# Feed-forward square on VectorE, an order planned with traced durations, and filler matmuls ahead of the feed-forward

## The chip, the cores and the metric

The kernel runs on one core of a Trainium2 chip. The metric is the device time of one execution in microseconds (us). The core's engines are called by the profile's names: PE (TensorE's matmul) and PEld (its weight load), DVE (VectorE), ACT (ScalarE), POOL (GpSimd), SP (SyncE, which here issues the DMAs).

## The reference

Thresholded attention over 8 batches of 8 heads (576 positions, head dimension 64), whose output is the input of a gated feed-forward layer with token shift (model width 512, hidden width 1024). q, k and v are float32, the feed-forward's weights float64.

```python
def _attn_ref(q, k, v, tau):
    scale = 1.0 / np.sqrt(q.shape[-1])
    scores = scale * np.matmul(q, k.transpose(0, 1, 3, 2))
    thresh = np.max(scores, axis=-1, keepdims=True) - tau
    scores = np.where(scores >= thresh, scores, -1000000000.0)
    scores = scores - np.max(scores, axis=-1, keepdims=True)
    attn = np.exp(scores)
    attn = attn / (np.sum(attn, axis=-1, keepdims=True) + 1e-09)
    return np.matmul(attn, v).astype(np.float32)

def _moe_ref(x, mu_k, mu_r, w_k, w_v, w_r):
    B, S, D = x.shape
    x_prev = np.concatenate([np.zeros((B, 1, D), dtype=np.float32), x[:, :-1, :]], axis=1)
    xk = mu_k * x + (1.0 - mu_k) * x_prev
    xr = mu_r * x + (1.0 - mu_r) * x_prev
    k = np.maximum(xk @ w_k, 0.0)
    v = k * k @ w_v
    r = 1.0 / (1.0 + np.exp(-(xr @ w_r)))
    return (r * v).astype(np.float32)
```

## The kernel before

**The plan.** The kernel doesn't issue instructions in the order in which its Python loops meet them. Each piece of work is a step, given to `add` with its engine, its cost (`occ`, how long the engine is held; `lat`, how long until the result can be used, `occ + 0.1` if not given), what it reads and writes, a priority `key` and a name `kind`. `Plan.order` then lays all steps out in a simulated time: at each turn it takes, over all engines, the step that can start earliest, and among steps of one engine that could start together the one with the smallest key. `Plan.issue` emits the instructions in that order, so that each engine's queue is fixed by the plan, while semaphores guard the data. The plan's numbers set only the order, and no engine waits for a planned time.

The key of a step is shifted by `NUDGE[kind]`, and by `FIRST[kind]` too while the key is below `UNTIL` (60). `HOP` is the planned delay from one engine to another, `LATE` an extra delay for the score and attention matmuls after `FROM` (200 us planned), `AHEAD` how far their keys are put forward. `CHUNK` and `FETCH` model PE's instruction fetch: 3.55 us for each 256 instructions.

**Attention.** A job is one pair of heads of one batch, 32 in all. `operands` loads rq, rk and v (L455 on) and makes the split operands qa, qb and kc: each float32 value is kept as a rounded part and the remainder. A job has five units (four of 128 queries by two heads, and "T" for the 64 queries left over of both heads). For a unit, `scores` runs the score matmuls into a PSUM tile `s` (L562, L578; three such tiles), and `softmax` takes the negated row maximum on DVE (L624, L632), the threshold on ACT (L640, Prelu with a huge slope), the exponential and its sum on ACT (L648), the reciprocal on DVE (L656, L657) and the normalisation on POOL (L671). `turn` transposes on DVE (L688, L692), and `attend` multiplies with v on PE in three groups of 96 small matmuls (L717), again into `s` tiles, which ACT copies into xT and xE (L743, L750).

**Weights.** `weight` makes 20 pieces (8 of w_k, 4 of w_r, 8 of w_v) during the first jobs: a DMA of 512 KB of float64 words on SP, an ACT pass (L397), four DVE passes that pick the bits together (L405 `dve5`, L419 `dve6`, L426 `dve7`, L436 `dve8`), an ACT copy (L443) and a POOL subtraction for the remainder (L447). `W0 + W1 * j` is the earliest planned time of the DMA of piece j of the first eight, `W2` of all later ones.

**Feed-forward.** `ffn_chunk` works on 256 positions: 18 chunks, two per batch and two for the left-over positions of four batches each. A chunk makes xk and xr (POOL subtraction L816, DVE scaling L825, ACT copy L838, POOL remainder L846), multiplies xk with w_k in four groups of 24 matmuls (L868, into one of the two PSUM tiles `w`), takes Relu (L876, ACT), the square (L877, ACT), its rounded part (L881, ACT) and remainder (L891, POOL) into k2; it multiplies xr with w_r (L910), applies the sigmoid on ACT (L914, L918), multiplies k2 with w_v (L932), and multiplies both on DVE (L938) before the output DMA. Tiles `r` (two) hold the intermediate values, and `k2` and `sg` exist once.

The square and its neighbours on ACT:

```python
add("ACT", 0.49, lambda r=r, h=h: A.activation(r.get(), h.get().rearrange("p a b -> p (a b)"), AF.Relu), reads=[h], writes=[r], key=key - 20, kind="act11")
add("ACT", 0.53, lambda r=r: A.activation(r.get(), r.get(), AF.Square), writes=[r], key=key - 1, kind="act12")
```

Of the kernel before, what the change touches and what calls it, by code (L numbers as in the profile page):

```python
# [7 lines left out]
F32 = mybir.dt.float32  # L8
FR = mybir.dt.float32r
# [40 lines left out]
class Plan:  # L50
# [3 lines left out]
    HOP, LATE, FROM, AHEAD = 0.05, 0.05, 200.0, 65.0  # L54
    SOFT = {"DVE": 0, "ACT": 0}
    NUDGE = {
# [7 lines left out]
    }  # L64
    FIRST, UNTIL = {
# [8 lines left out]
    CHUNK, FETCH = 256, 3.55  # L74
# [62 lines left out]
    def order(self, loose=()):  # L137
# [24 lines left out]
        code, turned = 0, -100.0  # L162
        out = []
# [86 lines left out]
    def issue(self):  # L250
        for i in self.out:
            self.steps[i].fn()
# [3 lines left out]
def tile_threshold_attention_then_rwkv_ffn(  # L256
# [45 lines left out]
    W0, W1, W2, W3, AVK = 3.220, 2.801, 34.671, 0.000, 1.0  # L302
# [67 lines left out]

    pieces = {}

    def weight(j, name, w, c, f, key, wait):
# [8 lines left out]
        def t():  # L382
            return xT[1].get()[:, col, 1 : 1 + 512]
# [12 lines left out]
            0.56,  # L396
# [3 lines left out]
            key=key, kind="act1",  # L400
# [3 lines left out]
            0.4,  # L404
            lambda: V.tensor_scalar(t(), t(), W_MIN, W_MAX, op0=ALU.max, op1=ALU.min),  # L405
            writes=box,
            key=key, kind="dve5",
# [5 lines left out]
        def word(y):  # L413
# [4 lines left out]
            0.4,  # L418
            lambda: V.tensor_scalar(u(), u(), 0x07FFFFFF, 3, op0=ALU.bitwise_and, op1=ALU.logical_shift_left),  # L419
            writes=box,  # L420
            key=key, kind="dve6",
# [3 lines left out]
            0.65,  # L425
# [5 lines left out]
            key=key, kind="dve7",  # L431
# [3 lines left out]
            0.65,  # L435
# [5 lines left out]
            key=key, kind="dve8",  # L441
        )
        add("ACT", 0.53, lambda: A.activation(piece.get()[:, 0], t(), AF.Copy), reads=box, writes=[(piece, 0)], key=key, kind="act2")  # L443
        add(
            "POOL",
            1.27,
# [3 lines left out]
            key=key, kind="pool1",  # L450
# [4 lines left out]
    def operands(job, key):  # L455
        b, hp = job["b"], job["hp"]
        job["st"] = []
        for h in range(2):
# [20 lines left out]
                0.62,  # L479
# [3 lines left out]
                key=key - PREP, kind="act4",  # L483
# [9 lines left out]
                key=key - PREP, kind="pool2",  # L493
# [3 lines left out]
                0.7,  # L497
# [5 lines left out]
                key=key - PREP, kind="act3",  # L503
# [3 lines left out]
                0.8,  # L507
# [10 lines left out]
                key=key - PREP, kind="dve7b",  # L518
# [13 lines left out]
    def scores(unit, ss, key):  # L532
# [5 lines left out]
        if unit["kind"] == "T":  # L538

            for v_ in range(2):  # L540
                for h in range(2):

                    def tail(v_=v_, h=h):
# [6 lines left out]
                        0.26,  # L550
# [3 lines left out]
                        key=key - 3, kind="act5",  # L554
# [33 lines left out]
    def softmax(unit):  # L588
# [16 lines left out]
        for y in ys:  # L605
# [12 lines left out]
            def col(j, y=y):  # L618
# [4 lines left out]
                0.67,  # L623
# [3 lines left out]
                key=key - KMAX, kind="dve9",  # L627
# [3 lines left out]
                0.1,  # L631
# [3 lines left out]
                key=key - KMAX, kind="dve10",  # L635
# [3 lines left out]
                0.625,  # L639
# [3 lines left out]
                key=key - KEXP, kind="act6",  # L643
# [3 lines left out]
                0.70,  # L647
# [3 lines left out]
                key=key - KMASK, kind="act7",  # L651
# [3 lines left out]
        def invert():  # L655
# [5 lines left out]
            0.29,  # L661
# [3 lines left out]
            key=n + 0.5, kind="dve11",  # L665
        )
        for y in ys:
            add(
                "POOL",
                0.715,  # L670
                lambda y=y: G.tensor_scalar(  # L671
                    part(y), part(y), sm.get()[:, 3, y : y + 1], 0.0, op0=ALU.mult, op1=ALU.add
                ),
                reads=[(sm, (3, y))],
                writes=[p[y]],
                key=n - 1.0, kind="pool3",
            )
# [4 lines left out]
    def turn(unit):  # L682
# [11 lines left out]
        if unit["kind"] == "P":  # L694
            add("DVE", 1.27, main, writes=[(sq, (c, 0)), (sq, (c, 1))], key=n - 1.0, kind="dve12")
        else:
            add("DVE", 0.7, tail, writes=[(sq, (c, 1))], key=n - 1.0, kind="dve13")

    def attend(job, key):
# [39 lines left out]
        for a in range(2):  # L739
# [16 lines left out]
            add("ACT", 0.3, put, reads=[os[a]], writes=main, key=key - 5, kind="act8")  # L756
            add("ACT", 0.1, put_tail, reads=[os[a]], writes=tail, key=key - 5, kind="act9")
# [15 lines left out]
    def ffn_chunk(kind, b0, g, key):  # L773
# [35 lines left out]
        for hc in range(0, NCT, 2):  # L809
# [9 lines left out]
            for j in range(2):  # L819
                d = sbuf("r", [P, 2, CH], F32, 2)  # L820

                def scale(j=j, d=d, diff=diff, hc=hc):
# [18 lines left out]
                    key=key, kind="act10",  # L841
# [9 lines left out]
                    key=key, kind="pool6",  # L851
# [4 lines left out]
        for j in range(NFT // 2):  # L856
            h = psum("w", [P, 2, CH], NF)
            for f in range(2):
# [17 lines left out]
            add("ACT", 0.49, lambda r=r, h=h: A.activation(r.get(), h.get().rearrange("p a b -> p (a b)"), AF.Relu), reads=[h], writes=[r], key=key - 20, kind="act11")  # L876
            add("ACT", 0.53, lambda r=r: A.activation(r.get(), r.get(), AF.Square), writes=[r], key=key - 1, kind="act12")  # L877
            add(
                "ACT",
                0.53,  # L880
# [5 lines left out]
                key=key - 1, kind="act13",  # L886
# [9 lines left out]
                key=key - 1, kind="pool7",  # L896
# [3 lines left out]
        for j in range(CH // P):  # L900
# [13 lines left out]
            add("ACT", 0.49, lambda j=j, z=z: A.activation(sg.get()[:, j], z.get(), AF.Copy), reads=[z], writes=[(sg, j)], key=key - 20, kind="act14")  # L914
        add(
            "ACT",
            3.6,
            lambda: A.activation(sg.get(), sg.get(), AF.Sigmoid),  # L918
            writes=[(sg, 0), (sg, 1)],
            key=key - 1, kind="act15",  # L920
        )
        for j in range(CH // P):
            ts = slice(j * P, (j + 1) * P)
            vps = psum("w", [P, DM], NF)
            for ft in range(NFT):
# [15 lines left out]
                key=key - 20, kind="dve15",  # L941
# [100 lines left out]
```

## Time and profile before

| what | value |
|---|---|
| median of three runs | 1008.28 us (1006.56 to 1009.07) |
| profiled execution | 1007.83 us, span 1005.8 us |
| PE busy | 900.2 us (90%), 13520 matmuls |
| ACT busy | 794.9 us (79%) |
| DVE busy | 705.8 us (70%) |
| POOL busy | 588.6 us (59%) |
| mean granted PE clock | 0.948 |

A group's row names its line, engine, operation, output and input, and then gives the busy time, the mean of one in ns, the idle time of the engine just before these instructions, and what ended it. A row of waits gives the waiting engine and line, the releaser, us in total, times and the longest. A row of the timeline gives start, duration, engine, line, operation and how many were merged, with the idle time before it in brackets. An engine that isn't the bottleneck may be idle at no cost.

### The profile page before, as it was taken

The numbers are of one execution on the slowest core, as the hardware profiler recorded it, in microseconds if no ns is written. First come the engines' busy times: TensorE is split into PE (matmuls) and PEld (weight loads), VectorE is DVE, ScalarE is ACT, GpSimd is POOL, SyncE is SP. The second block draws the span as 40 slices with busy tenths as digits, with TensorE's granted clock in tenths as the row PEclk, the third lists the DMA queues.
The fourth block names the chain that finished last, engine by engine and source line by source line (L and its number), as shares of the span: only waits on it lengthen the run. The fifth ranks groups of instructions, "written<-read, shape, count | busy, mean of one in ns | idle before, by whom it ended". The sixth has DMA issues, their size and how long they took to land.

```text
span 1005.8 us, 32052 instructions
## 1 busy us (share of the span) xinstructions
PE 900.2 (90%) x13520; PEld 790.3 (79%) x13520; DVE 705.8 (70%) x1434; ACT 794.9 (79%) x1660; POOL 588.6 (59%) x576
## 2 busy tenths in 40 slices
PE   3355669899989999999999999999999999999988
PEld 3244558798878988898889798888888888889876
DVE  5979999677878686868686958686858677741130
ACT  5766878788889898989898798888898979854422
POOL 1756667665656665756565657565666657543431
PEclk9577778899999999999999999999999999999999
DMA  7562231233323232333222223332322222210001
GB/s 282 179 252 82 89 105 50 72 117 103 110 96 117 96 117 96 117 97 103 98 99 91 77 76 117 96 117 84 118 72 89 94 90 73 70 49 22 22 22 22
DMA packets 31599, 97.48 MB, mean 97 GB/s; under 512 B 3808, under 2 KB 3808, under 8 KB 27360
## 3 DMA queue, kind: packets, MB, share of 16 engines
q1 hardware_dynamic: 31456, 95.44, 28.1%
q8 instruction: 106, 1.74, 0.7%
q14 instruction: 37, 0.30, 0.1%
HBM read 85.99 MB, written 9.44 MB: 95 GB/s over the span
## 4 chain that ended last, share of the span: by engine, by line
PE 43%; DVE 9%; ACT 4%; POOL 3%; issue 2%; ACTq 0%; DVEq 0%; POOLq 0%
PE w L868 13%; PE s L717 8%; PE w L932 7%; PE w L910 7%; PE s L578 6%; DVE r L825 3%; DVE sm L624 2%; DVE sq L688 2%; PE s L562 2%; POOL sq L671 1%; POOL xk L846 1%; ACT sq L640 1%; ACT sq L648 1%; ACT L648 1%; DVE sm L656 1%
## 5 line engine op out<-in xcount | busy, mean ns | idle before, releaser
L671 POOL TENSOR_SCALAR sq<-sq,sm 128x576 f32<-128x576 f32 x288 | 239.4, 843 | 162.4 <-DVE sm L657 90.6
L624 DVE TENSOR_REDUCE sm<-s 128x1 f32<-128x576 f32 x288 | 211.9, 745 | 81.6 <-PE s L578 75.7
L640 ACT ACTIVATE sq<-s,sm 128x576 f32<-128x576 f32 x288 | 206.4, 737 | 59.2 <-DVE sm L632 55.5
L868 PE MATMUL w<-xk,wk 128*128 128x256 f32 x1728 | 228.8, 285 | 4.0 <-ACT xk L838 2.3
L868 PEld LDWEIGHTS w<-xk,wk 128*128 128x128 f32 x1728 | 217.7, 191 | 9.6 <-issue 4.2
L648 ACT ACTIVATE sq<-sq,small 128x576 f32<-128x576 f32 x288 | 222.9, 777 | 2.0
L932 PE MATMUL w<-wv,k 128*128 128x512 f32 x864 | 215.2, 394 | 0.0
L688 DVE STREAM_TRANSPOSE sq<-sq 128x1152 f32<-128x1152 f32 x128 | 175.5, 1371 | 54.8 <-POOL sq L671 54.5
L717 PE MATMUL s<-sq,v 32*64 32x144 f32 x9216 | 177.8, 292 | 19.2 <-issue 8.4
L717 PEld LDWEIGHTS s<-sq,v 32*64 32x64 f32 x9216 | 151.0, 133 | 44.2 <-issue 23.8
L932 PEld LDWEIGHTS w<-wv,k 128*128 128x128 f32 x864 | 157.8, 188 | 32.5 <-issue 3.6
L578 PE MATMUL s<-kc,qa 128*128 128x288 f32 x512 | 128.4, 334 | 50.3 <-ACT sq L640 37.6
L578 PEld LDWEIGHTS s<-kc,qa 128*128 128x128 f32 x512 | 88.7, 204 | 78.0 <-ACT sq L640 35.2
L488 POOL TENSOR_TENSOR kc<-rk,kc 64x576 fp32r<-64x576 f32 x64 | 96.8, 1517 | 82.0 <-issue 60.8
L846 POOL TENSOR_TENSOR xk<-r,xk 128x512 fp32r<-128x512 f32 x72 | 95.3, 1324 | 83.8 <-ACT xk L838 82.8
L578 PE MATMUL s<-kc,qb 128*128 128x288 f32 x512 | 117.7, 314 | 0.0
L891 POOL TENSOR_TENSOR k<-r,k 128x512 fp32r<-128x512 f32 x72 | 93.2, 1298 | 40.1 <-ACT k L881 38.1
L910 PE MATMUL w<-wr,xk 128*128 128x512 f32 x432 | 107.1, 393 | 0.0
L825 DVE SCALAR_TENSOR_TENSOR r<-r,mu_sb,xT 128x256 f32<-128x256 f32 x128 | 73.9, 618 | 37.9 <-POOL xk L846 22.3
L578 PEld LDWEIGHTS s<-kc,qb 128*128 128x128 f32 x512 | 89.5, 205 | 1.2 <-issue 1.2
L910 PEld LDWEIGHTS w<-wr,xk 128*128 128x128 f32 x432 | 78.9, 189 | 14.5 <-ACT r L876 0.3
L838 ACT ACTIVATE xk<-r 128x512 fp32r<-128x512 f32 x72 | 45.2, 628 | 54.6 <-DVE r L825 54.3
(53 smaller groups left out, 915.2 us busy)
## 6 DMA issues: line engine op xcount, KB each, us to landing
v<-in_v SPq DMA_DIRECT2D x32, 1152.0 KB, 5.1
rq<-in_qk SPq DMA_DIRECT2D x64, 288.0 KB, 2.9
rk<-in_qk SPq DMA_DIRECT2D x64, 288.0 KB, 2.9
out<-sg SPq DMA_DIRECT2D x32, 256.0 KB, 2.1
wk<-in_w_k SPq DMA_DIRECT2D x8, 512.0 KB, 7.9
wv<-in_w_v SPq DMA_DIRECT2D x8, 512.0 KB, 10.5
wr<-in_w_r SPq DMA_DIRECT2D x4, 512.0 KB, 6.5
out<-sg SPq DMA_DIRECT2D x8, 128.0 KB, 2.4
```

Of the source, the lines that this page charges most:

```text
L578: PE.matmul(ss[y].get()[:, z, 0:HS], l.get()[:, c * P : (c + 1) * P], r.get()[:, keys(z)], start=(j == 0), stop=(j == 1),)
L624: lambda sv=sv, col=col: V.tensor_reduce(col(0), sv(), axis=AX.XY, op=ALU.max, negate=True),
L640: lambda st=st, pv=pv, col=col: A.activation(pv(), st(), AF.Prelu, bias=col(1), alpha=STEEP),
L648: lambda y=y, col=col: A.activation(part(y), part(y), AF.Exp, bias=small.get()[:, 3:4], accum_out=col(2)),
L671: lambda y=y: G.tensor_scalar(part(y), part(y), sm.get()[:, 3, y : y + 1], 0.0, op0=ALU.mult, op1=ALU.add),
L688: V.transpose(t, t)
L717: PE.matmul(os[a // 2].get()[hs, a % 2, 0:NX], vt.get()[rows, j, hs], sq.get()[rows, j, h], start=(j == 0), stop=(j == NB - 1),)
L825: V.scalar_tensor_tensor(d.get()[:, y, o : o + n], diff.get()[:, y, o : o + n], mu_sb.get()[:, j, hc + y : hc + y + 1], prv[:, hc + y], op ...
L846: lambda j=j, d=d, cs=cs: G.tensor_tensor(mix[j].get()[:, 1, cs], d.get(), mix[j].get()[:, 0, cs].bitcast(F32), op=ALU.subtract),
L868: PE.matmul(h.get()[:, f], l, r, start=(ct == 0 and i == 0), stop=(ct == NCT - 1 and i == 2))
L910: PE.matmul(z.get(), l, r, start=(ct == 0 and i == 0), stop=(ct == NCT - 1 and i == 2))
L932: PE.matmul(vps.get(), l, r, start=(ft == 0 and i == 0), stop=(ft == NFT - 1 and i == 2))
```

## The change

1. The square of the hidden values is a DVE product `r * r` (kind `dve16`) in place of an ACT activation.
2. The planned costs of many steps, `NUDGE`, `FIRST`, `LATE`, `AHEAD` and the planned times of the weight DMAs are set anew, so the order on every engine differs. Each weight's ACT and DVE passes, for example, now have a `lat` of their own.
3. Wherever the plan leaves PE idle for more than 0.3 us and no `w` tile has been used yet, it counts how many matmuls of 0.12 us fit in the gap; `issue` emits as many filler matmuls (128x128 by 128x256, all ones) at that place in PE's queue. They write to a tile `waste`, which lies where the second `w` tile will be.

```diff
-    HOP, LATE, FROM, AHEAD = 0.05, 0.05, 200.0, 65.0
+    HOP, LATE, FROM, AHEAD = 0.05, 0.1, 200.0, 70.0
     NUDGE = {
-        "act1": -59.5, "act10": 67.0, "act11": -222.0, "act12": -115.0, "act13": 59.5, "act14": -52.5, "act15": 165.0,
...
+        "act1": -76.0, "act10": 42.5, "act11": -241.5, "act12": -115.0, "act13": 28.5, "act14": -15.5, "act15": 189.0,
...
-    CHUNK, FETCH = 256, 3.55
+    CHUNK, FETCH, FILL = 256, 3.55, 0.12
...
+        self.fill = {}
...
             s.start = t
+            if e == "PE" and not turn["w"] and t - free[e] > 0.3:
+                self.fill[len(out)] = int((t - free[e]) / self.FILL)
...
     def issue(self):
-        for i in self.out:
+        for k, i in enumerate(self.out):
+            for _ in range(self.fill.get(k, 0)):
+                self.filler()
             self.steps[i].fn()
...
-    W0, W1, W2, W3, AVK = 3.220, 2.801, 34.671, 0.000, 1.0
+    W0, W1, W2, W3, AVK = 4.655, 3.665, 50.033, 0.000, 1.0
...
+    one = const.tile([P, CH], FR, name="one")
+    V.memset(one.bitcast(F32), 1.0)
+    waste = ps.tile([P, 512], F32, tag="w_1", name="waste", bufs=1)
+    plan.filler = lambda: PE.matmul(waste[:, 0:CH], one[:, 0:P], one, start=True, stop=True)
...
-            0.4,
+            0.333,
...
-            key=key, kind="dve5",
+            key=key, lat=0.42, kind="dve5",
...
-            0.4,
+            0.333,
...
-            key=key, kind="dve6",
+            key=key, lat=0.43, kind="dve6",
...
-            0.65,
+            0.6,
...
-            key=key, kind="dve7",
+            key=key, lat=0.69, kind="dve7",
...
-            0.65,
+            0.6,
...
-            key=key, kind="dve8",
+            key=key, lat=0.68, kind="dve8",
...
-            add("ACT", 0.49, ... AF.Relu), ... kind="act11")
-            add("ACT", 0.53, lambda r=r: A.activation(r.get(), r.get(), AF.Square), writes=[r], key=key - 1, kind="act12")
+            add("ACT", 0.478, ... AF.Relu), ... lat=0.6, kind="act11")
+            add("DVE", 0.6, lambda r=r: V.tensor_tensor(r.get(), r.get(), r.get(), op=ALU.mult), writes=[r], key=key - 1, lat=0.69, kind="dve16")
...
```

More of the change, by code (lines that the diff above doesn't have):

```diff
@@ L395, in weight @@
             "ACT",
-            0.56,
+            0.558,
             lambda: A.activation(t(), words.get()[:, :, 1].bitcast(F32), AF.Abs),
@@ L399, in weight @@
             writes=box,
-            key=key, kind="act1",
+            key=key, lat=0.67, kind="act1",
         )
@@ L440, in weight @@
             writes=box,
-            key=key, kind="dve8",
+            key=key, lat=0.68, kind="dve8",
         )
-        add("ACT", 0.53, lambda: A.activation(piece.get()[:, 0], t(), AF.Copy), reads=box, writes=[(piece, 0)], key=key, kind="act2")
+        add("ACT", 0.52, lambda: A.activation(piece.get()[:, 0], t(), AF.Copy), reads=box, writes=[(piece, 0)], key=key, lat=0.63, kind="act2")
         add(
             "POOL",
-            1.27,
+            1.24,
             lambda: G.tensor_tensor(piece.get()[:, 1], t(), piece.get()[:, 0].bitcast(F32), op=ALU.subtract),
@@ L449, in weight @@
             writes=[(piece, 1)],
-            key=key, kind="pool1",
+            key=key, lat=1.28, kind="pool1",
         )
@@ L478, in operands @@
                 "ACT",
-                0.62,
+                0.575,
                 lambda rk=rk, both=both: A.activation(both.get(), rk.get(), AF.Copy),
@@ L482, in operands @@
                 writes=[both],
-                key=key - PREP, kind="act4",
+                key=key - PREP, lat=0.68, kind="act4",
             )
@@ L492, in operands @@
                 writes=[both],
-                key=key - PREP, kind="pool2",
+                key=key - PREP, lat=1.44, kind="pool2",
             )
@@ L496, in operands @@
                 "ACT",
-                0.7,
+                0.667,
                 lambda rq=rq, top=top: A.activation(
@@ L502, in operands @@
                 writes=[top],
-                key=key - PREP, kind="act3",
+                key=key - PREP, lat=0.78, kind="act3",
             )
@@ L506, in operands @@
                 "DVE",
-                0.8,
+                0.726,
                 lambda rq=rq, top=top, low=low: V.scalar_tensor_tensor(
@@ L517, in operands @@
                 writes=[low],
-                key=key - PREP, kind="dve7b",
+                key=key - PREP, lat=0.81, kind="dve7b",
             )
@@ L549, in scores @@
                         "ACT",
-                        0.26,
+                        0.147,
                         tail,
@@ L626, in softmax @@
                 writes=[(sm, (0, y))],
-                key=key - KMAX, kind="dve9",
+                key=key - KMAX, lat=0.75, kind="dve9",
             )
@@ L634, in softmax @@
                 writes=[(sm, (1, y))],
-                key=key - KMAX, kind="dve10",
+                key=key - KMAX, lat=0.2, kind="dve10",
             )
@@ L642, in softmax @@
                 writes=[p[y]],
-                key=key - KEXP, kind="act6",
+                key=key - KEXP, lat=0.74, kind="act6",
             )
@@ L660, in softmax @@
             "DVE",
-            0.29,
+            0.28,
             invert,
@@ L664, in softmax @@
             writes=[(sm, (3, y)) for y in ys],
-            key=n + 0.5, kind="dve11",
+            key=n + 0.5, lat=0.47, kind="dve11",
         )
@@ L669, in softmax @@
                 "POOL",
-                0.715,
+                0.72,
                 lambda y=y: G.tensor_scalar(
@@ L675, in softmax @@
                 writes=[p[y]],
-                key=n - 1.0, kind="pool3",
+                key=n - 1.0, lat=0.76, kind="pool3",
             )
@@ L694, in turn @@
         if unit["kind"] == "P":
-            add("DVE", 1.27, main, writes=[(sq, (c, 0)), (sq, (c, 1))], key=n - 1.0, kind="dve12")
+            add("DVE", 1.292, main, writes=[(sq, (c, 0)), (sq, (c, 1))], key=n - 1.0, lat=1.38, kind="dve12")
         else:
-            add("DVE", 0.7, tail, writes=[(sq, (c, 1))], key=n - 1.0, kind="dve13")
+            add("DVE", 0.69, tail, writes=[(sq, (c, 1))], key=n - 1.0, lat=0.77, kind="dve13")
     def attend(job, key):
@@ L754, in put_tail @@
                 )
-            add("ACT", 0.3, put, reads=[os[a]], writes=main, key=key - 5, kind="act8")
-            add("ACT", 0.1, put_tail, reads=[os[a]], writes=tail, key=key - 5, kind="act9")
+            add("ACT", 0.265, put, reads=[os[a]], writes=main, key=key - 5, lat=0.39, kind="act8")
+            add("ACT", 0.077, put_tail, reads=[os[a]], writes=tail, key=key - 5, lat=0.2, kind="act9")
     def edge(b, key):
@@ L875, in ffn_chunk @@
             r = sbuf("r", [P, 512], F32, 2)
-            add("ACT", 0.49, lambda r=r, h=h: A.activation(r.get(), h.get().rearrange("p a b -> p (a b)"), AF.Relu), reads=[h], writes=[r], key=key - 20, kind="act11")
-            add("ACT", 0.53, lambda r=r: A.activation(r.get(), r.get(), AF.Square), writes=[r], key=key - 1, kind="act12")
+            add("ACT", 0.478, lambda r=r, h=h: A.activation(r.get(), h.get().rearrange("p a b -> p (a b)"), AF.Relu), reads=[h], writes=[r], key=key - 20, lat=0.6, kind="act11")
+            add("DVE", 0.6, lambda r=r: V.tensor_tensor(r.get(), r.get(), r.get(), op=ALU.mult), writes=[r], key=key - 1, lat=0.69, kind="dve16")
             add(
                 "ACT",
-                0.53,
+                0.52,
                 lambda r=r, js=js: A.activation(
@@ L885, in ffn_chunk @@
                 writes=[(k2, (0, j))],
-                key=key - 1, kind="act13",
+                key=key - 1, lat=0.63, kind="act13",
             )
@@ L895, in ffn_chunk @@
                 writes=[(k2, (1, j))],
-                key=key - 1, kind="pool7",
+                key=key - 1, lat=1.3, kind="pool7",
             )
@@ L913, in ffn_chunk @@
                 add("PE", 0.69, mm, reads=[w, *([xr] if ct == 0 else [(xr, (0, c2)), (xr, (1, c2))])], writes=[z, *([(sg, j)] if ct == 0 else [])], key=key, lat=0.86, kind="pe7", ni=6)
-            add("ACT", 0.49, lambda j=j, z=z: A.activation(sg.get()[:, j], z.get(), AF.Copy), reads=[z], writes=[(sg, j)], key=key - 20, kind="act14")
+            add("ACT", 0.478, lambda j=j, z=z: A.activation(sg.get()[:, j], z.get(), AF.Copy), reads=[z], writes=[(sg, j)], key=key - 20, lat=0.6, kind="act14")
         add(
             "ACT",
-            3.6,
+            3.55,
             lambda: A.activation(sg.get(), sg.get(), AF.Sigmoid),
             writes=[(sg, 0), (sg, 1)],
-            key=key - 1, kind="act15",
+            key=key - 1, lat=3.65, kind="act15",
         )
@@ L940, in ffn_chunk @@
                 writes=[(sg, j)],
-                key=key - 20, kind="dve15",
+                key=key - 20, lat=0.68, kind="dve15",
             )
```

16 lines of the change are left out of this document (8 added, 8 removed), and 27 rows, old and new, of the table NUDGE.

## The prediction, made before the changed kernel ran

> **What bounds the kernel now.** I read the stages first: busy time of each engine by stretch. The cut at 153 us is where the first feed-forward matmul (L868) runs, and the cut at 900 where attention is nearly over. The columns are the stretch, its length, busy us of PE, PEld, DVE, ACT and POOL, the granted clock, the DMA share and GB/s.
>
> ```profile
> 0.00:153.00 153.00, 77.64 (x1366) 64.89 (x1367) 133.90 (x253) 110.76 (x236) 83.80 (x80) 0.73 0.46 163
> 153.00:200.00 47.00, 43.43 (x672) 38.27 (x671) 37.61 (x74) 38.88 (x82) 35.51 (x32) 0.89 0.18 62
> 200.00:900.00 700.00, 681.94 (x10757) 601.61 (x10755) 515.83 (x1056) 608.59 (x1284) 433.59 (x431) 1.00 0.29 96
> 900.00:1006.00 106.00, 97.24 (x731) 85.50 (x729) 18.42 (x54) 36.69 (x60) 35.70 (x35) 0.97 0.07 21
> ```
>
> There are two regimes. Up to 153 us DVE is busy 88% of the time and PE only 51%, at a granted clock of 0.73. From 200 us on PE is busy 97% at full clock, with 18.1 us idle in 700. So a gain has three places: an earlier start of the feed-forward, the 18.1 us, and PE's 8.8 us idle in the last stretch. Anything else falls on engines that wait for PE. The second view is who waits for whom, for PE up to 153 us (two lines), for DVE there (one), for PE from 200 to 900 us (six) and at the end (two).
>
> ```profile
> PE s L578 <- ACT sq L640: 32.5, 18, 9.3
> PE s L717 <- issue: 6.7, 4, 3.9
> ...
> DVE sm L624 <- PE s L578: 10.0, 5, 5.0
> ...
> PE s L578 <- ACT sq L640: 5.1, 9, 0.9
> PE s L717 <- ACT sq L640: 4.5, 4, 2.2
> PE s L578 <- ACT xT L743: 2.4, 5, 0.8
> PE s L717 <- ACT r L877: 2.2, 1, 2.2
> PE s L717 <- issue: 1.2, 2, 1.0
> PE s L717 <- ACT sq L648: 0.9, 1, 0.9
> ...
> PE w L868 <- ACT xk L838: 2.3, 1, 2.3
> PE w L868 <- POOL xk L846: 1.7, 2, 1.0
> ```
>
> Early on, PE's waits are for PSUM tiles that DVE and ACT free, so they are DVE's pace seen from PE. Only where DVE itself waits for PE (10.0 us of its 19.1 idle) does PE's speed count. The largest of these is in the timeline, with two bursts of the attention product for the clock:
>
> ```profile
> 47.90 3.13 PE L717 MATMUL s<-sq,v 32*64 32x144 f32 x96
> 429.25 1.78 PE L717 MATMUL s<-sq,v 32*64 32x144 f32 x96
> 59.98 0.46 PE L717 MATMUL s<-sq,v 32*64 32x144 f32 x4 [3.93 <-issue]
> 61.21 0.76 DVE L624 TENSOR_REDUCE sm<-s 128x1 f32<-128x576 f32 x1 [4.97 <-PE s L578]
> ```
>
> The same 96 matmuls take 3.13 us at the half clock that follows an idle stretch, and 1.78 us in the dense stage. DVE's hole of 4.97 us stands behind such a burst and behind 3.93 us of PE waiting for its own instructions.
>
> **The change part by part.** The sum is against the profiled execution: 1007.83 us, its span 1005.8 and 2.0 around it; the median of the runs, 1008.28, lies 0.45 above.
>
> *Fillers.* Their price is that of the feed-forward's equal shape, dense and full clock against cold:
>
> ```profile
> 911.52 11.58 PE L868 MATMUL w<-xk,wk 128*128 128x256 f32 x96
> 922.95 5.63 PE L910 MATMUL w<-wr,xk 128*128 128x512 f32 x24
> 152.60 1.48 PE L868 MATMUL w<-xk,wk 128*128 128x256 f32 x6
> 154.13 0.85 PE L578 MATMUL s<-kc,qa 128*128 128x288 f32 x2
> ```
>
> From start to the next start that is 11.43/96 = 0.119 us warm, which is the plan's 0.12, and 1.53/6 = 0.255 cold. PE's real work up to 153 us is about 77.64 x 0.73 = 57 us at full clock, so some 96 us of gaps hold about 800 fillers, 1600 instructions with their weight loads. As long as they end before the real step's operand is there they cost nothing; what covers them is DVE. Their gain lies in DVE's waits for PE. Bounds: 10.0 us gained if all of them go, and a loss that I price under the rivals. I take half, -5, because the largest wait is part clock (3.13 against 1.78) and part instruction fetch, which a full clock doesn't help. The clock also still stands at 0.73 when the feed-forward begins, and at 0.70 in a second cold stretch:
>
> ```profile
> 152.60:160.00 7.40, 7.35 (x45) 7.05 (x45) 6.71 (x18) 6.53 (x17) 5.83 (x6) 0.73 0.21 76
> 180.00:190.00 10.00, 7.06 (x28) 6.16 (x27) 6.00 (x14) 4.89 (x14) 6.16 (x6) 0.70 0.19 63
> ```
>
> Here PE is busy throughout, so the first gives 7.35 x 0.27 = 2.0 us; fillers end with the first feed-forward matmul, so the second (2.1 us) stays. -2. The plan counts its fetch chunks of 256 without the fillers, so the four fetch waits (6.7 us) fall elsewhere: between -6.7 and +6.7, taken as 0, since nothing in the rows favours either phase. The tile `waste` lies in a feed-forward PSUM slot, and whatever follows in it is PE's own, in order. The memset of `one` is half the size of this one, and DVE then waits for a transfer anyway:
>
> ```profile
> 0.97 0.48 DVE L363 MEMSET bd<- 128x512 f32 x1
> 3.31 0.15 DVE L331 TENSOR_SCALAR small<-small 128x1 f32<-128x1 f32 x1 [1.85 <-DMA small<-in_tau]
> ```
>
> It costs nothing; without that cover about 0.25 us.
>
> *Square from ACT to DVE.* The rows: the square on ACT, a DVE product with one operand in PSUM, and two DVE operations with two operands in SBUF (min/median/max in ns where three numbers stand).
>
> ```profile
> L877 ACT ACTIVATE r<-r 128x512 f32<-128x512 f32 x72 | 45.4, 630 | 0.6
> L938 DVE TENSOR_TENSOR sg<-w,sg x36: 643/678/693, 200.5 to 1001.2; 128x512 f32<-128x512 f32 x36
> L825 DVE SCALAR_TENSOR_TENSOR r<-r,mu_sb,xT x128: 443/479/1660, 94.6 to 941.4; 128x256 f32<-128x256 f32 x128
> L825 DVE SCALAR_TENSOR_TENSOR r<-r,mu_sb,xT 128x256 f32<-128x256 f32 x128 | 73.9, 618 | 37.9 <-POOL xk L846 22.3 <-POOL r L816 15.6
> L436 DVE SCALAR_TENSOR_TENSOR xT<-wk,xT x8: 669/682/1881, 25.5 to 84.2; 128x512 uint32<-128x512 uint32 x8
> L436 DVE SCALAR_TENSOR_TENSOR xT<-wk,xT 128x512 uint32<-128x512 uint32 x8 | 6.8, 846 | 0.0
> ```
>
> ACT loses 72 x 0.630 = 45.4 us. A DVE product of this size takes 0.678 us, and operations with both operands in SBUF are now and then stretched: L825 has a mean of 0.618 over a least of 0.443, 0.175 more or 1.4 times, L436 0.846 over 0.669. L938, with one operand in PSUM, never is. The square reads r twice from SBUF. Its price lies between 0.678 (no stretch) and 0.678 x 1.4 = 0.95; I take 0.678 + 0.175 = 0.85, since L436, the same width, shows that much added. 72 of them are 61 us, where the plan counts 0.6 each, 43. The feed-forward runs from 153 to 1006, so 700/853 of the 72, about 59, fall between 200 and 900 us. There ACT goes from 87% to (608.6 - 59 x 0.63)/700 = 82%, DVE from 74% to (515.8 + 59 x 0.85)/700 = 81%. Of PE's 18.1 us idle there 15.1 end with ACT. Bounds: all of them gained, or as much again added, because DVE's queue is in order and a square waiting for its Relu holds the reductions behind it, which hold ACT. I take -7 for about half of ACT's and +3 for DVE's: -4. The chain Relu, square, copy, low half gains one more change of engine; its cover is the gate's product (L910, 5.63 us a chunk) between the last L868 group and L932, while the chain without its last piece, Relu, square and copy, is about 0.63 + 0.85 + 0.63 = 2.1 us, taking ACT's two at L877's price; so 3 us are left for the low half on POOL.
>
> The Trainium skill, SBUF — State Buffer, section Who interferes with whom, says that a VectorE instruction with two SBUF inputs contends with a GpSimd instruction reading SBUF; the trace agrees (L436 up to 1881 ns, L938 never over 693). By the plan's 0.6 the DVE share would be 79%, by the stretched row 81%; either leaves PE the bound.
>
> *Order.* All priorities, costs and the LATE and AHEAD terms change what stands next to what. The trace of before can't show the new order, so it is bounded by what an order can recover: up to 153 us the DVE idle not caused by PE, 19.1 - 10.0 = 9.1 us (part of it the first loads), and at the end PE's 4.0 us for xk. As loss the same 13 us. I take -2, nearest to the 4.0. The weight transfers move later on SP's queue: the last wk from 3.22 + 7 x 2.801 = 22.8 to 30.3 us, the wr and wv from 34.7 to 50. The L436 row shows wk pieces consumed until 84.2, so it costs 0. If DVE took the pieces as they come, up to 7.5 us would show.
>
> Sum: -5 - 2 - 4 - 2 = -13, so 1007.8 - 13 = 994.8, and 995 beside the median.
>
> **The rivals.** *A larger gain from order, 981.* DVE does more before 153 us than the first feed-forward matmul needs:
>
> ```profile
> L624 DVE TENSOR_REDUCE sm<-s 128x1 f32<-128x576 f32 x47 | 34.5, 744 | 10.9 <-PE s L578 10.0 <-PE s L562 0.9
> L405 DVE TENSOR_SCALAR xT<-xT 128x512 f32<-128x512 f32 x17 | 11.9, 720 | 0.0
> L419 DVE TENSOR_SCALAR xT<-xT 128x512 uint32<-128x512 uint32 x17 | 10.7, 644 | 0.0
> L426 DVE SCALAR_TENSOR_TENSOR xT<-wk,xT 128x512 uint32<-128x512 uint32 x8 | 6.3, 795 | 0.0
> ```
>
> Seventeen weight pieces where 8 are needed, at 0.72 + 0.64 + 0.80 + 0.85 = 3.0 us each, is 27 us. It must be done soon after, so I credit half: 13.5 beyond the forecast, 981. Against it: PE then reaches wr and wv before they are there.
>
> *No change, 1008.* DVE hides the clock gain and PE's density hides ACT's relief; each of the four terms is then under 1 us. For it: DVE 88% busy early. Against: 10.0 us of DVE's idle there does end on PE.
>
> *Slower, the fillers make PE late, 1023.* They fill every planned gap, so PE has no slack left before the feed-forward. If three tenths of the 800 run cold, PE falls 0.3 x 800 x (0.255 - 0.12) = 32 us behind the plan. DVE itself falls behind the plan by its stretched operations, whose planned times to the result are 0.42, 0.43, 0.68 and 0.69 us: 17 x (0.72 - 0.42) + 17 x (0.64 - 0.43) + 17 x (0.80 - 0.68) + 17 x (0.85 - 0.69) = 13 us, which is cover; 19 remain, and with the square's -4 that is 1007.8 + 19 - 4 = 1023. It turns to a loss above 13 + 4 = 17 us of lateness, 16% of the fillers cold. Against it: cold stretches follow idle ones, and fillers leave none.
>
> *Slower, squares stretched in DVE's queue, 1013.* If each stretch (0.175 us x 72 = 12.6) comes out at PE, as a reduction or a square that is late for it, ACT's relief is lost, and only the clock's -5 - 2 stays: 1007.8 + 12.6 - 7 = 1013. It decides from 7 us, 40 of the 72 stretches. For it: DVE's queue is in order and 81% full. Against it: PE's waits in the dense stage end with ACT (15.1 of 18.1), which is relieved. The Trainium skill's rule of the shared port, above, is what would bring such stretches.
>
> **How the numbers follow.** Within 0.3% is 1005.3 to 1011.3, about what a measurement of this kernel can tell from no change. Forecast 0.50 (its own range 986 to 1004), larger gain 0.17, no change 0.11, late fillers 0.12, stretched squares 0.10. Hence faster 0.67, same 0.11, slower 0.22. The range 976 to 1015 leaves out about 0.07 of the larger gains and 0.12 on the slow side.
>
> **What would show it.** The granted clock up to the first L868 near 0.95 and PE's busy share there near 90%; the first L868 at 145 to 149 us; DVE's wait for L578 there near 5 us; ACT near 750 us busy in all, DVE near 767, the square's mean 0.80 to 0.90 us; PE's idle from there to 900 near 14 us. I am wrong if the first L868 comes after 155 us, if PE's waits in the dense stage now end with DVE, or if the squares wait long for Relu with reductions behind them.

## The result and the profile after

| kernel | median, us | ratio to the kernel before | 95% interval |
|---|---|---|---|
| before (8 runs beside the changed kernel) | 1008.43 | | |
| changed (8 runs) | 1013.43 | 1.0052 | 1.0038 to 1.0066 |

The changed kernel is slower by half a per cent, 5.0 us, where 995 was forecast. The profiled execution took 1013.79 us, its span 1012.0. Busy in all: PE 949.8 us (528 of its 14048 matmuls are fillers), ACT 756.4, DVE 767.1, POOL 608.1. The stages, with the same columns as before:

```profile
0.00:153.00 153.00, 129.81 (x1904) 121.18 (x1904) 132.09 (x252) 108.36 (x230) 88.01 (x78) 0.96 0.47 166
153.00:200.00 47.00, 41.72 (x682) 35.28 (x689) 43.99 (x82) 39.60 (x85) 38.47 (x34) 1.00 0.18 61
200.00:900.00 700.00, 675.48 (x10893) 594.03 (x10889) 562.68 (x1107) 576.14 (x1222) 441.66 (x428) 1.00 0.29 96
900.00:1012.00 112.00, 102.78 (x580) 90.32 (x578) 28.34 (x69) 32.26 (x50) 39.98 (x38) 0.98 0.06 19
```

The clock up to 153 us rose from 0.73 to 0.96, as wanted, yet DVE was busy there for 132.1 us against 133.9, and the first feed-forward matmul came at 151.5 us against 152.6: the early work hardly got further. In the dense stage ACT fell from 608.6 to 576.1 us and PE still lost: its idle time rose from 18.1 to 24.5 us. The waits say where. For DVE up to 153 us (one line) and for PE from 200 to 900 (three), then PE's wait for the transpose in the kernel before:

```profile
DVE sm L635 <- PE s L589: 12.0, 4, 5.9
...
PE s L589 <- ACT sq L651: 11.4, 16, 1.8
PE s L728 <- DVE sq L699: 6.9, 6, 1.7
PE s L728 <- issue: 1.4, 1, 1.4
```

```profile
PE s L717 <- DVE sq L688: 0.4, 1, 0.4
```

DVE's waits for PE grew from 10.0 to 12.0 us. In the dense stage a new line stands second: the attention product waits 6.9 us for the transpose on DVE, where it was 0.4 in one wait before.

### The profile page after: what moved, and what is told of

It reads as the page before. It is cut to its first block, busy times and chain, and to the rows that moved or that the text cites. A ratio compares the mean times of both kernels' runs of the same rounds, so it can differ in the third digit from the quotient of the medians.

```text
span 1012.0 us, 33088 instructions
## 1 busy us (share of the span) xinstructions
PE 949.8 (94%) x14048; PEld 840.8 (83%) x14048; DVE 767.1 (76%) x1507; ACT 756.4 (75%) x1586; POOL 608.1 (60%) x576
## 4 chain that ended last, share of the span: by engine, by line
PE 44%; DVE 32%; POOL 8%; ACT 8%; issue 6%; POOLq 0%; ACTq 0%; DVEq 0%
PE s L728 11%; PE w L879 10%; PE w L943 9%; DVE sm L635 8%; PE s L589 7%; DVE sq L699 7%; POOL sq L682 6%; PE w L921 5%; DVE r L836 4%; DVE qb L519 3%; ACT sq L651 2%; ACT sq L659 2%; DVE sm L667 2%; DVE sm L643 2%; PE waste L380 1%
## 5 line engine op out<-in xcount | busy, mean ns | idle before, releaser
L682 POOL TENSOR_SCALAR sq<-sq,sm 128x576 f32<-128x576 f32 x288 | 256.2, 900 | 153.1 <-DVE sm L668 105.5
L699 DVE STREAM_TRANSPOSE sq<-sq 128x1152 f32<-128x1152 f32 x128 | 175.7, 1373 | 60.4 <-POOL sq L682 59.9
L589 PE MATMUL s<-kc,qa 128*128 128x288 f32 x512 | 122.5, 321 | 29.0 <-ACT sq L651 24.2
L499 POOL TENSOR_TENSOR kc<-rk,kc 64x576 fp32r<-64x576 f32 x64 | 99.4, 1556 | 75.9 <-issue 47.0
L589 PEld LDWEIGHTS s<-kc,qa 128*128 128x128 f32 x512 | 82.6, 190 | 57.7 <-ACT sq L651 32.9
L589 PE MATMUL s<-kc,qb 128*128 128x288 f32 x512 | 110.5, 298 | 0.0
L888 DVE TENSOR_TENSOR r<-r 128x512 f32<-128x512 f32 x72 | 54.1, 751 | 39.0 <-ACT r L887 38.9
```

Source lines behind the costliest of these rows:

```text
L499: lambda rk=rk, both=both: G.tensor_tensor(both.get()[D:P], rk.get()[D:P], both.get()[D:P].bitcast(F32), op=ALU.subtract),
L589: PE.matmul(ss[y].get()[:, z, 0:HS], l.get()[:, c * P : (c + 1) * P], r.get()[:, keys(z)], start=(j == 0), stop=(j == 1),)
L682: lambda y=y: G.tensor_scalar(part(y), part(y), sm.get()[:, 3, y : y + 1], 0.0, op0=ALU.mult, op1=ALU.add),
L699: V.transpose(t, t)
```

## The experiments

Names: the *new order* is the changed kernel's plan, the *old order* that of before. Where the square is edited, the plan stays and only the instruction that its step emits is another; the edits of fillers and transfers are shown with their runs. Letters of theories are those of the expectations. Each group was timed beside the kernel before (medians 1008.1 to 1009.0), so ratios are what is compared; 0.1% is 1.0 us. Where two intervals overlap, the difference between the two rows is not clear of the noise, and the text says so.

| order | fillers | square | other | median, us | ratio | interval |
|---|---|---|---|---|---|---|
| new | none | DVE, r * r | | 1011.18 | 1.0028 | 1.0016 to 1.0040 |
| new | all | ACT | | 1013.54 | 1.0045 | 1.0031 to 1.0060 |
| old | none | DVE, r * r | | 1022.43 | 1.0139 | 1.0121 to 1.0158 |
| old | all | ACT | | 1010.48 | 1.0020 | 1.0008 to 1.0032 |
| new | all | left out | | 1003.11 | 0.9933 | 0.9916 to 0.9951 |
| old | none | left out | | 1006.11 | 0.9971 | 0.9960 to 0.9983 |
| old | none | DVE, h * r | | 1019.09 | 1.0106 | 1.0080 to 1.0133 |
| new | none | DVE, r * r | transfers spread | 1008.70 | 0.9994 | 0.9984 to 1.0003 |
| old | none | ACT | transfers spread | 1004.54 | 0.9967 | 0.9953 to 0.9981 |
| new | first gap cut | DVE, r * r | | 1008.20 | 0.9999 | 0.9985 to 1.0013 |
| new | all | DVE, h * r | | 1006.78 | 0.9987 | 0.9973 to 1.0002 |
| new | first gap cut | DVE, h * r | transfers spread | 999.16 | 0.9910 | 0.9892 to 0.9929 |
| new | first gap cut | ACT | | 1007.08 | 0.9988 | 0.9974 to 1.0001 |
| new | none | DVE, h * r | transfers spread | 1003.10 | 0.9945 | 0.9928 to 0.9962 |
| old | first gap cut | ACT | transfers spread | 1001.54 | 0.9944 | 0.9925 to 0.9963 |

### Order, square and fillers apart

*New order, no fillers.*

```diff
-            if e == "PE" and not turn["w"] and t - free[e] > 0.3:
+            if False:
```

> The changed kernel with its own order and the square on DVE, but no filler matmuls. Theory O (the order of the dense stage loses the time): without fillers the start runs at a low clock again, DVE's early work hides it, 1013 us give or take 3. Theory S (the square on DVE loses it): the same, 1013 give or take 3. Theory F (the fillers make PE late): back to 1005 to 1009. If the fillers are worth what the prediction said (5 to 7 us): 1018 to 1020.

1011.18 us: inside the range of theories O and S (1010 to 1016) and above that of F. Against the changed kernel the fillers cost 0.24% (the two intervals just touch). The worth that the prediction put on them, 1018 to 1020 us without them, is refuted.

*New order, the square on ACT.*

```diff
-  lambda r=r: V.tensor_tensor(r.get(), r.get(), r.get(), op=ALU.mult)
+  lambda r=r: A.activation(r.get(), r.get(), AF.Square)
```

> The changed kernel with its order and fillers, only that the instruction of the square's step is issued on ACT (630 ns) in place of DVE; every queue keeps its sequence otherwise. Theory S (the square on DVE, its load and its stretches, makes PE wait in the dense stage): 1004 to 1008, with PE's waits for the transpose (6.9 us) gone. Theory O (the order loses the time whoever squares): 1013 to 1022, since ACT now has work that the order did not count on it.

1013.54: no difference from DVE, though PE's waits for the transpose fell from 6.9 to 3.5 us. I read it as theory O then; the runs without a square showed that this was too quick.

*Old order, the square on DVE* (the reverse edit on the kernel before).

> The kernel before with its order, only that the square's instruction is issued on DVE. Theory S: 1012 to 1018, PE's idle time from 200 to 900 us up from 18 to 25 us or more. Theory O: 1003 to 1009, since ACT, which ended 15 of the 18 us of PE's waits, is relieved.

1022.43, slower than either theory gave. In an order that expects it on ACT, a DVE square costs 1.4% more than one on ACT.

*Old order with fillers* (the change's filler code added to the kernel before, 590 matmuls).

> The kernel before with its order and its square on ACT, plus the filler matmuls in the gaps that its own plan leaves before the first feed-forward matmul. Theory O and theory S both have the fillers harmless: 1003 to 1008 with the clock near 1.0 up to 153 us (at most the 2 us of the first feed-forward stretch and a little of DVE's waits gained). Theory F: 1012 or more.

1010.48, between the two ranges: they cost 0.20% here, about the same as in the new order. Read beside the new order with its square on ACT (1013.54, also with all fillers), the new order is 0.25% slower than the old when both square on ACT; the two intervals just touch.

### The square left out, and with one operand in PSUM

```diff
-  lambda r=r: V.tensor_tensor(r.get(), r.get(), r.get(), op=ALU.mult)
+  lambda: None
```

> The changed kernel (its order, its fillers) with the square left out on every engine, so the hidden value goes on as Relu alone; all queues are otherwise in sequence. Theory L (work: in the dense stage a square costs PE time on whichever engine it stands): 1003 to 1007, PE's idle time from 200 to 900 us down from 24 to 15 us or less. Theory O (the new order itself is too tight, and PE waits for transposes and scores with or without a square): 1009 to 1013, PE's idle time there still 18 us or more.

> The kernel before with the square left out. Theory L: 1002 to 1005, PE's idle time from 200 to 900 us from 18 to about 12. Theory O: the same order of size, 1003 to 1008; read beside the changed kernel without a square it gives what the two orders are worth with equal work: under theory O the old order's dense stage is still 6 us or more ahead.

1003.11 and 1006.11. Theory O falls by the times: with no square the new order is the faster one. Theory L is right for the new order's time only. PE's idle time from 200 to 900 us fell from 24.5 to 18.5 us there, not to 15, and in the old order from 18.1 to 17.2, not to 12; and 1006.11 lies outside L's 1002 to 1005. So a square costs each order something else: the new order pays 1.1 to 1.2% for it on either engine, the old one 0.3% for a square on ACT.

```diff
-  lambda r=r: V.tensor_tensor(r.get(), r.get(), r.get(), op=ALU.mult)
+  lambda r=r, h=h: V.tensor_tensor(r.get(), h.get().rearrange("p a b -> p (a b)"), r.get(), op=ALU.mult)
```

h * r with r = max(h, 0) is the same square, but one operand is read from PSUM.

> The kernel before with the square's step issued on DVE as h times r, one operand in PSUM and one in SBUF, against r times r (1022.4 us). If the stretching beside POOL is what costs (rival of stretched squares): square mean near 0.68 in place of 0.79 us and 1013 to 1017. If it is the square's place and load in DVE's queue: 1020 to 1024.

1019.09 in the old order, between the two ranges. By the medians 0.33% of the 1.39% is the second SBUF operand, though the two intervals overlap; the groups changed clearly, the square from a mean of 793 to 676 ns and POOL's normalisation from 869 to 842 (843 with the square on ACT). The rest is put down to the square's place in queues that were laid out without it.

> The changed kernel with the square as h times r, one operand in PSUM. If stretching beside POOL is part of what the square costs in the new order too, as it was in the old one (3.3 us): square mean 0.68 in place of 0.75 us, 1009 to 1011. If the square's place in DVE's queue is all: 1013 to 1014.

1006.78 in the new order, 0.65% less than r * r and more than I expected. The groups of the square and of POOL's normalisation, in the changed kernel, then with h * r, then POOL's in the kernel before:

```profile
L888 DVE TENSOR_TENSOR r<-r 128x512 f32<-128x512 f32 x72 | 54.1, 751 | 39.0 <-ACT r L887 38.9
L682 POOL TENSOR_SCALAR sq<-sq,sm 128x576 f32<-128x576 f32 x288 | 256.2, 900 | 153.1 <-DVE sm L668 105.5
```

```profile
L888 DVE TENSOR_TENSOR r<-w,r 128x512 f32<-128x512 f32 x72 | 49.1, 682 | 39.5 <-ACT r L887 39.4
L682 POOL TENSOR_SCALAR sq<-sq,sm 128x576 f32<-128x576 f32 x288 | 245.2, 862 | 152.0 <-DVE sm L668 110.6 <-DVE sm L643 19.8 <-ACT xT L408 10.2
```

```profile
L671 POOL TENSOR_SCALAR sq<-sq,sm 128x576 f32<-128x576 f32 x288 | 239.4, 843 | 162.4 <-DVE sm L657 90.6 <-DVE sm L632 29.6 <-ACT k L881 12.4
```

With two SBUF operands the square is stretched by 0.07 us on average, 5 us in all; but POOL's normalisation takes 0.038 us longer each, 11 us in all, and DVE's transposes wait for it (59.9 us on POOL against 53.1). The 843 ns belong to the old order, so they are no measure for this: in the new order the group had 871 ns with the square on ACT. In the old order the two parts were about equal, 8.4 us on the square and 7.7 on POOL. Which of the two PE feels was not separated. PE's waits from 200 to 900 us with h * r:

```profile
PE s L589 <- ACT sq L651: 10.1, 13, 1.8
PE w L879 <- DVE r L888: 3.3, 3, 1.3
...
PE s L728 <- DVE sq L699: 0.8, 2, 0.4
```

The wait for the transpose falls from 6.9 to 0.8 us. In its place 3.3 us come up, where PE waits for a PSUM tile until the square has read it. The 39 us that DVE stands idle at the squares until their Relu is done are the same with both forms (38.9 and 39.4), so they are no part of the gain.

### The first gap

The timeline of PE, first in the changed kernel, then in the new order without fillers, then with the first gap cut:

```profile
1.18 11.42 PE L380 MATMUL waste<-one 128*128 128x256 f32 x72 [1.18 <-DVE one L378]
12.44 0.69 PE L573 MATMUL s<-kc,bd 128*128 128x288 f32 x4
```

```profile
10.20 1.33 PE L573 MATMUL s<-kc,bd 128*128 128x288 f32 x4 [10.20 <-POOL kc L499]
```

```profile
1.19 7.07 PE L380 MATMUL waste<-one 128*128 128x256 f32 x45 [1.19 <-DVE one L378]
10.22 0.80 PE L573 MATMUL s<-kc,bd 128*128 128x288 f32 x4 [1.96 <-POOL kc L499]
```

In the kernel before, the same operand ended PE's first wait:

```profile
PE s L562 <- POOL kc L488: 10.3, 1, 10.3
```

Without fillers the first score matmul starts as its operand arrives, at 10.20 us. The 72 fillers of the first gap run until 12.4 us, so the score matmul is 2.2 us late and the first reduction comes with it. In three other profiled executions of the new order with 72 fillers it started between 11.4 and 12.2 us.

```diff
-                self.fill[len(out)] = int((t - free[e]) / self.FILL)
+                self.fill[len(out)] = min(int((t - free[e]) / self.FILL), 45 if not free[e] else 999)
```

> The changed kernel with the fillers of the first gap alone cut from 72 to 45, so that they end before the first score matmul's operand is there (10.2 us without fillers, 12.4 us with them); all other fillers stay. If the fillers' cost (2.2 us) is the late first score: first score matmul near 10.3 us, the first reduction 1.2 us or more earlier, 1011 to 1012. If it lies in the later fillers (fetch, PE late in the later gaps): 1013 to 1014.

1008.20: 0.53% gained by 27 matmuls fewer, more than the 2.2 us that the late score alone explains. DVE's holes behind PE, in the changed kernel and with the cut:

```profile
13.70 1.42 DVE L635 TENSOR_REDUCE sm<-s 128x1 f32<-128x576 f32 x2 [5.07 <-PE s L589]
84.28 0.76 DVE L635 TENSOR_REDUCE sm<-s 128x1 f32<-128x576 f32 x1 [5.88 <-PE s L589]
```

```profile
11.72 0.76 DVE L635 TENSOR_REDUCE sm<-s 128x1 f32<-128x576 f32 x1 [3.09 <-PE s L589]
79.47 1.42 DVE L635 TENSOR_REDUCE sm<-s 128x1 f32<-128x576 f32 x2 [2.04 <-PE s L589]
```

The second hole shrinks by 3.8 us as well. It stands in an attention product of 288 matmuls, in which PE stops for something that is no semaphore (`issue`). PE's rows of that product, in the changed kernel and with the cut:

```profile
71.15 1.25 PE L728 MATMUL s<-sq,v 32*64 32x144 f32 x60
75.75 3.65 PE L728 MATMUL s<-sq,v 32*64 32x144 f32 x128 [3.34 <-issue]
81.67 0.46 PE L728 MATMUL s<-sq,v 32*64 32x144 f32 x4 [2.27 <-issue]
```

```profile
70.19 1.69 PE L728 MATMUL s<-sq,v 32*64 32x144 f32 x87
74.83 2.49 PE L728 MATMUL s<-sq,v 32*64 32x144 f32 x105 [2.95 <-issue]
```

Counted from the start of the program, the first stop comes after 860 of PE's matmuls in both kernels, and the changed kernel's second one 128 later, after 988. With 27 fillers fewer the same counts fall 27 matmuls later in the work (87 of the product's matmuls in place of 60 before the first stop), so that 988 lies behind the product's end, among fillers, and no stop shows there. A second effect of the cut is thus where the stops fall, and that they fell well is luck: no run kept the count and removed only the late start. The two effects together are in DVE's waits for PE up to 153 us, 12.0 us in the changed kernel, 9.6 without fillers and 7.0 with the cut, and the times stand in the same order. Against no fillers at all (1011.18), the fillers outside the first gap are worth 0.3% (the intervals just part), the moved stops included.

### The transfers in a row

Why PE stops in that product is the next question. The new order's SP queue issues all twelve w_r and w_v transfers together, and behind them the DMA share is full while PE makes the two stops shown above. SP's rows, and the share by stretch of 10 us (last but one number):

```profile
58.67 1.91 SPq L399 DMA_DIRECT2D wr<-in_w_r  x4
60.63 8.09 SPq L399 DMA_DIRECT2D wv<-in_w_v  x8
```

```profile
60.00:70.00 10.00, 9.26 (x124) 8.68 (x128) 9.38 (x25) 9.91 (x21) 5.55 (x5) 1.00 1.01 396
70.00:80.00 10.00, 6.06 (x240) 5.16 (x223) 7.92 (x14) 3.58 (x11) 5.74 (x6) 0.83 0.95 375
```

The hole of the kernel before (3.93 us at 59.98) follows its own such row, issued from 42 to 51.5 us. The edit leaves the plan alone and emits two of these transfers at their first place and two behind each load that follows on the queue:

```diff
+        late = [i for i in self.out if steps[i].kind == "dma2"][8:]
...
+            if late and i not in before and room == 0:
+                room = 2
+                out += [late.pop(0), late.pop(0)]
+            out.append(i)
+            if i not in before and steps[i].eng == "DMA" and late:
+                out += late[:2]
+                del late[:2]
```

> The changed kernel without fillers (1011.2 us), with one edit: the twelve weight transfers that its queue issues in a row (w_r and w_v) go out two behind each following load. Theory W (PE's instruction fetch, and with it the DVE hole near 75 to 85 us, stands behind those 6 MB): the fetch waits of PE up to 153 us under 2 us, 1006 to 1009. Rival (the hole is DVE's and ACT's own): unchanged, 1010 to 1013.

> The kernel before with one edit: the twelve w_r and w_v transfers, issued in a row from 42 us, go out two behind each following load. Theory W (PE's instruction fetch stands behind those 6 MB and makes DVE's 4.97 us hole): the 3.93 us fetch wait gone, DVE's waits for PE up to 153 us from 10.0 to 6 us or less, 1003 to 1006. Rival: unchanged, 1007 to 1010.

1008.70 and 1004.54: 0.34% and 0.33% gained, and both times are those that theory W expected. Its other signs came in part: in the new order a stop of 2.4 us stays at a later score matmul, where under 2 us were expected, and in the old order DVE's waits for PE fell from 10.0 to 6.6 us, not to 6. In the old order the wait inside the same product falls from 3.93 to 1.14 us (L737 is L717 there):

```profile
56.66 0.46 PE L737 MATMUL s<-sq,v 32*64 32x144 f32 x4 [1.14 <-issue]
```

That the waits are PE's fetch of instructions is inferred. The profile says that no semaphore ended them, that they shrink or go when the transfers are spread, and that they stand at fixed counts: after 220 and 348 matmuls in the kernel before, 604 in the new order without fillers, 860 and 988 in the changed kernel, all multiples of 128 apart, which with one weight load for each matmul are 256 instructions. That holds for the stops of 0.5 us and more in the first 90 us; later ones fit it less well, and the 2.4 us at the score matmul do not fit it.

### Together, and what was still open

> Three edits on the changed kernel together: first gap's fillers cut to 45, weight transfers two behind each load, square as h times r. If they add up (1.5 to 2, 2.5 and 3 us): 1005 to 1008, the kernel before or a little under it. If they take the same slack: 1009 to 1011.

999.16, ratio 0.9910, well below both ranges, since the single gains were larger than the expectation took them: together the three edits gain 1.42% on the changed kernel, and singly 0.53, 0.34 (measured without fillers) and 0.65%, 1.52% in all. Its stages:

```profile
0.00:153.00 153.00, 130.55 (x1934) 121.11 (x1935) 139.70 (x270) 116.33 (x246) 95.52 (x85) 0.99 0.47 167
153.00:200.00 47.00, 44.32 (x764) 36.97 (x763) 42.25 (x77) 39.71 (x87) 35.28 (x33) 1.00 0.27 89
200.00:900.00 700.00, 679.86 (x10817) 598.19 (x10816) 551.50 (x1100) 571.80 (x1211) 431.98 (x428) 1.00 0.29 94
```

DVE does 7.6 us more work before 153 us than in the changed kernel, and the first feed-forward matmul comes at 141.6 us against 151.5 (before: 152.6).

> The changed kernel with the first gap's fillers cut to 45 and the square's instruction issued on ACT. It repeats the comparison of the two engines with the late first score taken out of both. If engine and order are separate things: 1008, like the square on DVE with the same cut (1008.2), so that the new order has no room for an ACT square. If the late first score hid ACT's advantage: 1004 or less, and then the square's move is what costs.

1007.08 against 1008.20 for r * r: the intervals overlap, so with the late score out of the comparison there is still no clear difference between the engines, as long as both operands lie in SBUF. The square's move alone, r * r, gains nothing in the order that was made for it.

> The version with three edits (fillers cut in the first gap, transfers two behind each load, square as h times r; 999.2 us), without any fillers. Apart from the first gap the fillers were worth 3 us (1008.2 against 1011.2): if that holds, 1002. If with the transfers spread a warm clock has nothing left to save: 999 to 1000.

> The kernel before, its order and its square on ACT, with spread transfers (1004.5 us) and fillers cut to 45 in the first gap. If the fillers are worth 3 us in any order: 1001 to 1002. If the front of the old order hides them, as DVE was busy 88% there: 1004 to 1005. The new order's best is 999.2, so what remains between the two is what the order with the square on DVE brings.

1003.10 and 1001.54: once the first gap is cut, the fillers are worth 0.35% in the new order and 0.23% in the old one, where 1004.54 stood without them. The first difference is just at the edge of its intervals, the second inside them. The best of the new order is 0.34% under the best of the old, again at the edge.

## Why the prediction was wrong, by its own steps

**Fillers, -5: the step that failed first.** It said that they cost nothing as long as they end before the real step's operand is there, and left the condition unchecked at the one place where the trace of before could answer it: its first wait, 10.3 us for POOL's kc, tells when the operand comes. The plan's gap there held 72 fillers, and at the plan's 0.12 us these take 8.6 us from 1.2 us on and would have ended in time; they took 11.4 us. Both filler terms together, -5 and the clock's -2, came out at +2.4 us. The clock at 0.96 was right; the cut of 27 fillers, which takes away the late start and moves PE's stops, gains 5.3 us, and with it the rest of the fillers is worth 3 us in place of 7. The rival of late fillers had the place right (slow matmuls ahead of real ones in PE's order) and its price wrong: it took a share of 800, and there were 528, of which those of the first gap mattered.

**DVE's largest wait.** The prediction split the 4.97 us between clock and instructions and took half as gained. The runs with spread transfers show that the hole stands behind the row of transfers, which costs 0.33% in the old order and 0.34% in the new one (measured without fillers). So moving these transfers did cost nothing, as the prediction said; what it missed is that the hole would move with them, its start from 56 us to 78, and at 5.88 us would be no shorter. The 0 that it took for PE's fetch waits holds in their sum up to 153 us (6.7 us before, 6.4 after), but the cut shows that where they fall counts for DVE.

**Clock at the first feed-forward matmuls, -2.** They did run at the full clock: the first 12 took 1.59 us, against 2.76 without fillers. From 153 to 200 us the clock went from 0.89 to 1.00, but it stands at 1.00 there without fillers too, so there they weren't needed, and the second cold stretch, which was to stay, is gone in the new order. What this is worth by itself isn't shown; from 153 to 200 us PE is idle for 5.3 us against 3.6 before.

**Square, -4.** The relief of ACT was real (38.5 us less busy in all, 32.5 of them between 200 and 900) and worth nothing at PE. The stretch was over-estimated on DVE (0.751 us measured, 0.85 taken) and left out on POOL, where it adds 11 us in this order. Measured, r * r in place of h * r costs 0.65%, 6.6 us, on the wrong side of the term. The Trainium skill, SBUF — State Buffer, section Who interferes with whom, on which the prediction drew, calls the shared ports an exclusive lock, and says that the order of issue, not the shape of the operation, decides who is blocked; the POOL group at 900 ns against 862, and 869 against 842 in the old order, agrees that POOL is held up too. The rival "stretched squares, 1013" named this mechanism, with a price on DVE's side that was too high and none on POOL's. That its time came is luck, since it counts 7 us of gain from the clock that did not come. Two of the prediction's signs of being wrong came in part: 6.9 us of PE's waits in the dense stage end with DVE's transposes, and the squares wait 38.9 us in all for their Relu, 0.54 us each. Whether reductions stood behind them was not looked at.

**Order, -2.** It has no one price. With the square left out of both, the new order, its fillers and late first score included, is 0.38% faster than the old; with the square on ACT in both, and fillers in both, it is 0.25% slower; and with r * r on DVE in both, without fillers, it is 1.1% faster (1.0028 against 1.0139). A sum of separate terms for square and order could not hold this.

**The sum.** Without fillers the changed kernel is 0.28% slower than the kernel before, +2.8 us, where -6 was forecast for square and order. The fillers add 2.4 us, where -7 was forecast. With the runs that leave out the square, the same 0.52% reads -0.38 (the orders without a square) + 1.19 (a square in the new order) - 0.29 (in the old); these are differences of the same four ratios and add up by construction. Of the 1.19%, 0.65% goes with the second SBUF operand and 0.54% stays with h * r. So the second step that failed is the square's: it counted ACT's relief as a gain at PE, and the runs show that the new order has less room for a square than the old one, on either engine. Why its 0.54% with h * r is more than the old order's 0.29% on ACT was not taken apart further.

## What to carry to other kernels

Work that fills a planned gap is free only if it runs as fast as the plan counts; check the first gap against the traced arrival of the operand and leave the last microseconds of it empty. A filler also moves everything that goes by the count of instructions, so a small change of their number can gain or lose for another reason than the one it was made for. An operation with two SBUF operands on DVE can have a price on POOL too, and here one operand read from PSUM took most or all of it away. When bulk transfers are moved, ask what else stands still at that time, above all a long run of short matmuls. And the price of a piece of work is not a constant to add up: the same square cost 0.3% in one order and 1.2% in another.

## What the runs showed of the hardware that was not expected

At the start the matmuls ran slower than the printed clock says. The fillers alone in stretches of 2 us of the changed kernel (the stretch, its length, PE busy and count, PEld, clock, DMA share, GB/s):

```profile
3.00:5.00 2.00, 2.00 (x12) 2.00 (x11) 1.00 0.99 322
5.00:7.00 2.00, 2.00 (x11) 2.00 (x11) 1.00 1.02 250
7.00:9.00 2.00, 2.00 (x19) 2.00 (x18) 1.00 0.97 396
9.00:11.00 2.00, 2.00 (x20) 2.00 (x18) 1.00 0.96 400
```

Up to 7 us 11 to 12 fillers are counted in 2 us, afterwards 19 to 20 (a filler that a stretch cuts counts in both), with the clock column at 1.00 throughout. From start to start that is 0.213 us in the trace until 6.9 us, and 0.120 us from then on. This is why 72 of them took 11.4 us and not the plan's 72 x 0.12 = 8.6. What slows them is not shown: the DMA share is near 1 on both sides of the step. The place of the step differs from execution to execution, from 4.3 to 7.1 us in the nine profiles with fillers that were compared (4.3 and 7.1 in two with the cut), so the plan can't know when a given count of fillers ends.
